# One 2 MB transfer of weights cut into four of eight rows and one of 96, once in a decode kernel

## The chip, the cores and the metric

The kernel runs on one core of one Trainium2 chip. The metric is the device time of one execution in microseconds; the time before is the median of three runs.

## The reference

Two identical layers, each a block of attention over a cached context and a gated feed-forward network, for a batch of two with one new token each. Everything is float32.

```python
x = x + attention(layernorm(x), k_cache, v_cache, wq, wo)   # layer 0
x = x + reglu(layernorm(x), W_gate, W_up, W_down)
x = x + attention(layernorm(x), k_cache, v_cache, wq, wo)   # layer 1, the same arrays again
x = x + reglu(layernorm(x), W_gate, W_up, W_down)
# attention: 32 query heads on 8 kv heads, 32768 cached positions, head size 128
#   scores = q k^T / sqrt(128); p = softmax(scores); o = p v; out = o @ wo
# x [2, 1, 512], k_cache and v_cache [2, 8, 32768, 128], wq [512, 4096], wo [4096, 512]
# reglu: gate = h @ W_gate, up = h @ W_up, (relu(gate) * up) @ W_down, inner size 1792
```

The keys and values are 268 MB each, and both layers read all of them.

## The kernel before

The sixteen pairs of batch element and kv head are walked one after another, each in one *lap*. A lap's keys and values come as four halves, two of k and two of v, each a tile of 128 rows by 16384 floats (8.39 MB; 64 KB a row). Three slots `X`, `Z`, `Y` of that size in the store `arena` hold them; a slot is loaded again when TensorE (PE) has used what was in it.

Layer 0 walks the pairs upwards, layer 1 downwards. In a lap (`lap` in the code) PE first multiplies the second half of the values of the pair before (`values`, into `acc`), then the keys of its own pair (`keys`, into `scores`, named `pair` in the profile), then comes the softmax, then the first half of its values. Between the keys stand small matmuls by which the finished head goes through its part of the weights `wo` into `op` (`head_out`, `project`).

Those weights are the "way out". A tile of 2 MB, 128 rows by 4096 floats (16 KB a row), holds them for two kv heads; it lies at `WO_AT` and is called `weights` and `other` by halves. In laps 3, 7 and 11 of layer 0 (counted from 0, so `i % 4 == 3`; the last lap is excluded) and at three places in layer 1, `fetch_out` loads such a tile. GpSimd (POOL) copies one half over the other in the laps between. The first and last weights come in tiles of half the size.

All loads but x's are issued by SyncE (SP) in the order in which the code names them. SP waits where a transfer would overwrite what is still read, so what stands behind it on SP waits too. Every transfer has a *lane*, a semaphore that tells of its landing: `slot...` for the halves, `wo` for these weights, and otherwise the next of sixteen (`lane0` to `lane15`). A recorder (`Tape`) works out the waits from the regions that are read and written. A k half that goes into the first slot names `weights` as well (`also`), so its issue waits until the weights before it have landed; later readers of the weights then need no wait of their own. PE, VectorE (DVE) and ScalarE (ACT) run the laps as a hardware loop; SP's transfers are written out one by one.

x itself comes as two transfers of four rows by 128 floats on ACT's queue, at the start. At the end of a layer stand the feed-forward network's weights (`wgu`, `wd`), loaded in pieces through a ring or into free slots; at the end of the program the last pieces of `wd` land, PE multiplies, DVE adds to `xq` and SP stores it to `out`.

The profile names tiles and lines by the recorder: nearly all operations have line 214, so groups are told apart by their tiles.

Of the kernel before, what the change touches and what calls it, by code (L numbers as in the profile page):

```python
# [11 lines left out]
P = 128  # L12
# [9 lines left out]
EPS = 1e-5  # L22
QZ = 60
NLAYER = 2

# [5 lines left out]
LANES = 16  # L33
# [11 lines left out]
P_AT, MT_AT, ACS_AT, WO_AT = FLOW, FLOW + 2 * D, FLOW + 2 * D + 32, FLOW + 3 * D + 32  # L45
WO = 4 * D
# [262 lines left out]
def attention_reglu_decode(nc, hold, x, k, v, wq, wo, wgu, wd, out):  # L309
    tape = Tape(nc)  # L310
    pe, dve, act, pool, sp = map(tape.engine, ("tensor", "vector", "scalar", "gpsimd", "sync"))

    def sbuf(name, width):
        return hold.enter_context(nc.sbuf_tensor(name, [P, width], F32))[:, :]
# [4 lines left out]
    arena = sbuf("arena", ARENA)  # L319
# [9 lines left out]
    def tile(at, width):  # L329
        return arena[:, at : at + width]  # L330
# [8 lines left out]
    turn = [0, FLOW, 0, RING[0]]  # L339
# [13 lines left out]
    def fetch(at, src, lane=None, also=()):  # L353
        t = arena[:, at : at + src.shape[-1]]
        if lane is None:
            lane = f"lane{turn[2] % LANES}"
            turn[2] += 1
        sp.dma_start(t, src, lane=lane, also=also)
        return t

    def half(src, n, h, at, also=()):
        return fetch(at, src[n, h], f"slot{at // ROW}", also)
# [1 line left out]
    def part_of(src, n, h, lo, hi, at):  # L364
        return fetch(at, src[n, h, :, lo * D : hi * D])

    def fetch_out(h, n, t, lane="wo"):
        return fetch(t.offset, wo[:, h * WO : (h + n) * WO], lane)

    dve.memset(xq, 0.0)  # L370
    for b in range(NB):
# [104 lines left out]
    def place_queries(n, step=0):  # L476
        dve.tensor_copy(qz[:, 28 : 28 + REP], moving(lambda turn: bass.AP(
            qT.tensor, qT.offset + (1 + n) * REP + turn * (step * REP), [qT.ap[0], [1, REP]])))
# [8 lines left out]
    def soft_max(scores=scores):  # L487
        m1, nm, rs = own(0), own(1), own(2)
        dve.tensor_reduce(m1, scores, AX.XY, ALU.max)
        mt = tile(MT_AT, 32)  # L490
        dve.tensor_scalar_mul(mt, pair, m1)
        pe.matmul(small[0][:, :32], same, mt, start=True, stop=True)
        dve.tensor_reduce(nm, small[0][:, :32], AX.X, ALU.max, negate=True)
        act.activation(tile(P_AT, 2 * D), scores.rearrange("p a b -> p (a b)"), AF.Exp, bias=nm, scale=1.0, accum_out=rs)

    def soft_tail():
        pT, p = tile(PT_AT, 2 * D), tile(P_AT, 2 * D)
        for B in range(2):
            dve.transpose(pT[:, B * D : (B + 1) * D], p[:, B * D : (B + 1) * D])
        pe.matmul(small[1][:, 0:1], same, own(2), start=True, stop=True)  # L500
        dve.reciprocal(own(3), small[1][:, 0:1])
# [11 lines left out]
    def evacuate(split=True):  # L513
        acs = tile(PT_AT if split else ACS_AT, D)
        w = P if split else D
        for t in range(0, D, w):
            dve.tensor_scalar_mul(acs[:, t : t + w], acc[:, t : t + w], own(3))
        return acs

    def head_out(b, acs, weights=None):  # L520
        for t in range(4):
            pe.matmul(small[0][:, :REP], acs[:, t * P : (t + 1) * P], selh[:, 4 * t : 4 * t + 4], start=t == 0, stop=t == 3)
        if weights is not None:
            project(weights)
            dve.memset(oT, 0.0)
        dve.tensor_copy(moving(lambda turn: bass.AP(oT.tensor, oT.offset + (turn + b) % NB, [oT.ap[0], [NB, REP]])), small[0][:, :REP])
# [67 lines left out]
    dve.tensor_reduce(total[:, :1], xq, AX.X, ALU.add)  # L594
    for L in range(NLAYER):
        last = L == NLAYER - 1
        step = -1 if last else 1
# [7 lines left out]
        def keys(h, t, first=0, scores=scores):  # L605
            for e in range(0, t.shape[-1] // D, 8):
                k_blocks(h + e, t[:, e * D : min(t.shape[-1], (e + 8) * D)], first, scores)
                yield e

        def values(lo, t, first=False, final=False):  # L610
            n = t.shape[-1] // D
            for e in range(0, n, 8):
                v_blocks(lo + e, lo + min(e + 8, n), t[:, e * D : min(e + 8, n) * D], first and e == 0, final and e + 8 >= n)

        def lap(i, second, k_first):

            values(HALF, second or half(v, seq[i - 1], 1, b), False, True)
            evacuate(False)
            for e in keys(0, k_first or half(k, seq[i], 0, a, (weights,) if i > L else ())):
                if e == 8:  # L620
                    head_out(1, tile(ACS_AT, D), weights)
            if not last and i == NG - 1:
                pool.tensor_copy(tile(RING[1], KEPT), tile(a, KEPT))
            for _ in keys(HALF, half(k, seq[i], 1, c)):
                pass
            soft_max()
            soft_tail()
            values(0, half(v, seq[i], 0, a), True)
            place_queries(seq[L] + step, step)
            if i % 2 == 1 and i > 1 and (last or i + 1 < NG):  # L630
                h = seq[i] // NB
                if h == 0:
                    fetch_out(h, 1, weights)
                elif i % 4 == 3:
                    fetch_out(h - last, 2, tile(WO_AT, 2 * WO))
                else:
                    pool.tensor_copy(weights, other)

# [7 lines left out]
        if last:  # L646
            n, e = divmod(KEPT, D)

            def again(col):
                return a + col - KEPT if col < REST * D else RING[0] + LENT + col - REST * D  # L650

            for lo, hi in AGAIN:
                fetch(again(lo), k[seq[0], 0, :, lo:hi])
            k_blocks(0, tile(RING[1], n * D), NT // 2, gu)
            k_blocks(n, tile(RING[1] + n * D, e), NT // 2, gu, (0, e))
            k_blocks(n, tile(again(KEPT), D - e), NT // 2, gu, (e, D))
            for lo in range(n + 1, HALF):
                for _ in range({12: 3, REST: 2, 26: 2}.get(lo, 0)):
                    warm(448)
                if lo == REST + 4:  # L660
                    put_back(LENT, STASH)
                k_blocks(lo, tile(again(lo * D), D), NT // 2, gu)
            ready = {1: (tile(b, ROW), half(k, seq[1], 0, a))}
            fetch_out(seq[0] // NB, 1, weights)
            warm(448)
            warm(448)
            soft_max(gu)
            soft_tail()
            values(0, tile(c, ROW), True)
            place_queries(seq[1])  # L670
        else:
            ready = {0: (tile(b, ROW), None)}
            fetch_out(0, 1, weights)
            dve.memset(tile(PT_AT, 2 * D), 0.0)
            nothing(acc, True)
        for i in tape.laps(range(L, NG), 1):
            lap(i, *ready.pop(i, (None, None)))
        nothing(op, False)
        combine()
        n = seq[NG - 1]  # L680
        for lo, hi in ENDING if last else FLOWN:
            t = fetch(b + lo * D, v[n, 1, :, lo * D : hi * D])
# [44 lines left out]
```

## Time and profile before

| | |
|---|---|
| time, median of 3 runs | 2556.62 us (2556.6 to 2557.2) |
| the profiled execution: time, span | 2556.55 us, 2555.2 us |
| PE busy, share of the span | 1335.5 us, 52% |
| DVE, ACT, POOL busy | 157.0, 60.4, 18.2 us |
| bytes moved, mean rate | 1103.29 MB, 432 GB/s |
| the 2 MB loads of `wo`, issue to landing | 6 of them, 31.5 us (median) |

The page shows busy time by engine and, in a section of its own, by DMA queue: q1 is SP's, q10 is ACT's (x), q8 and q14 fetch instructions. A queue's share is the time that its packets took, as a share of what the 16 DMA engines have in that stretch; it can pass 100% where packets reach over the window's edge. A packet is one row (up to 64 KB) or the four bytes that tell of the end. The views of queues and engines can be asked for any window of the span. No view names the DMA engine that carried a packet.

### The profile page before, as it was taken

The page shows a single profiled execution, that of the slowest core. Times are in us where ns is not written, and L with a number is a line of the kernel's source. Part 1 is how long each engine was busy: PE and PEld are TensorE (multiplying, and loading weights), DVE is VectorE, ACT ScalarE, POOL GpSimd, SP SyncE. Part 2 cuts the span into 40 slices and gives each one's busy share as a digit, 9 for nine tenths or more (in the row PEclk, how much of TensorE's full clock was granted, in tenths as well). Part 3 has the DMA queues.
Part 4 walks back from the last instruction along what each step waited for, and adds up shares of the span by engine and source line. Part 5 has one row for each costly group of instructions (what it writes and reads, how often), then busy time and mean ns, then how long its engine had stood idle before and what let it go on. Part 6 is the DMA issues. An engine that isn't in the chain of part 4 may idle for free.

```text
span 2555.2 us, 20572 instructions
## 1 busy us (share of the span) xinstructions
PE 1335.5 (52%) x9542; PEld 366.1 (14%) x9542; DVE 157.0 (6%) x409; ACT 60.4 (2%) x82; POOL 18.2 (1%) x25
## 2 busy tenths in 40 slices
PE   4554545455444554455586554455445554455456
PEld 1111111111111111111121111111111111111112
DVE  1000000000000000000111000000000000000001
ACT  0000000000000000000000000000000000000000
POOL 0000000000000000000000000000000000000000
PEclk9677777777777777777798777777767777777778
DMA  9999999999999999999999999999999999999999
GB/s 425 429 440 429 427 441 430 440 430 431 436 430 440 430 438 429 430 440 430 425 423 440 434 435 432 431 435 435 434 433 431 436 433 435 432 432 435 433 435 389
DMA packets 27248, 1103.29 MB, mean 432 GB/s; under 512 B 3033, under 2 KB 3169, under 8 KB 8033
## 3 DMA queue, kind: packets, MB, share of 16 engines
q1 hardware_dynamic: 27216, 1103.06, 99.9%
q8 instruction: 12, 0.20, 0.0%
q14 instruction: 4, 0.02, 0.0%
q10 hardware_dynamic: 16, 0.00, 0.0%
HBM read 1102.99 MB, written 0.07 MB: 432 GB/s over the span
## 4 chain that ended last, share of the span: by engine, by line
DMA 73%; PE 26%; issue 0%; SPq 0%; DVE 0%; ACT 0%; ACTq 0%
DMA arena<-k 37%; DMA arena<-v 34%; PE acc L214 12%; PE pair L214 11%; DMA arena<-wd 1%; PE small L214 1%; PE op L214 1%; DMA arena<-wq 1%; DMA arena<-wgu 1%; SPq L214 0%; DVE stat L214 0%; DVE arena L214 0%; DVE xq L214 0%; ACT arena L214 0%; ACTq L295 0%
## 5 line engine op out<-in xcount | busy, mean ns | idle before, releaser
L214 PE MATMUL acc<-arena 128*16 128x512 f32 (+2 forms) x4288 | 612.1, 726 | 531.8 <-DMA arena<-v 522.0
L214 PE MATMUL pair<-arena,qz 128*32 128x512 f32 x4098 | 590.7, 730 | 557.5 <-DMA arena<-k 557.5
L214 PEld LDWEIGHTS pair<-arena,qz 128*32 128x32 f32 x4098 | 151.5, 131 | 987.0 <-issue 697.2
L214 PEld LDWEIGHTS acc<-arena 128*16 128x16 f32 (+1 forms) x4288 | 136.8, 112 | 970.6 <-issue 595.5
L214 ACT ACTIVATE arena<-pair,stat 128x1024 f32<-128x1024 f32 x32 | 35.7, 1114 | 2388.1 <-DVE stat L214 2388.1
L214 DVE TENSOR_SCALAR arena<-acc,stat 128x512 f32<-128x512 f32 (+1 forms) x39 | 25.5, 667 | 1051.3 <-PE acc L214 1051.3
L214 DVE TENSOR_REDUCE stat<-pair 128x1 f32<-128x1024 f32 x32 | 39.2, 1225 | 633.5 <-PE pair L214 633.5
L214 DVE STREAM_TRANSPOSE arena<-arena 128x512 f32<-128x512 f32 (+1 forms) x68 | 43.4, 674 | 40.8 <-ACT arena L214 40.7
L214 PE MATMUL small<-stat,cst 128*128 128x1 f32 (+1 forms) x72 | 16.6, 300 | 48.7 <-ACT arena L214 48.7
L214 PE MATMUL small<-arena,cst 128*128 128x32 f32 x64 | 13.1, 286 | 51.6 <-DVE arena L214 51.6
L214 PEld LDWEIGHTS small<-cst,arena 128*128 128x128 f32 x264 | 32.1, 191 | 28.7 <-issue 27.0
L214 PE MATMUL small<-cst,arena 128*128 128x4 f32 x264 | 35.0, 256 | 0.5 <-DVE arena L214 0.5
L214 PE MATMUL op<-arena,oT 128*2 128x512 f32 (+1 forms) x312 | 34.4, 526 | 0.4 <-DVE oT L214 0.3
L214 DVE MEMSET oT<- 128x8 f32 x33 | 2.1, 65 | 513.4 <-PE op L214 513.4
L214 POOL COPY arena<-arena 128x2048 f32<-128x2048 f32 (+1 forms) x7 | 13.5, 1923 | 2191.2 <-PE op L214 2046.7
L214 PE MATMUL op<-arena 128*32 128x448 f32 (+1 forms) x128 | 22.7, 573 | 3.0 <-DMA arena<-wq 1.4
L214 PEld LDWEIGHTS small<-stat,cst 128*128 128x128 f32 x72 | 13.6, 236 | 56.9 <-ACT arena L214 52.2
L214 PEld LDWEIGHTS small<-arena,cst 128*128 128x128 f32 x64 | 9.5, 188 | 80.5 <-DVE arena L214 80.5
L214 ACT ACT_TABLE_LOAD x16 | 20.5, 1283 | 11.4 <-DMA xq<-x 11.1
L214 PE MATMUL acc<-cst 128*32 128x448 f32 (+1 forms) x48 | 18.3, 480 | 0.0
L214 PE MATMUL small<-cst,stat 128*128 128x2 f32 x8 | 1.7, 286 | 18.6 <-DVE stat L214 18.1
L214 PE MATMUL small<-arena 128*32 128x128 f32 x224 | 9.0, 277 | 3.1 <-DVE arena L214 1.7
(63 smaller groups left out, 98.6 us busy)
## 6 DMA issues: line engine op xcount, KB each, us to landing
arena<-wo SPq DMA_DIRECT2D x6, 2048.0 KB, 31.5
arena<-v SPq DMA_DIRECT2D x2, 4096.0 KB, 37.4
arena<-wq SPq DMA_DIRECT2D x14, 512.0 KB, 6.4
arena<-wgu SPq DMA_DIRECT2D x10, 448.0 KB, 6.7
arena<-wo SPq DMA_DIRECT2D x4, 1024.0 KB, 25.3
arena<-wgu SPq DMA_DIRECT2D x1, 3584.0 KB, 44.6
arena<-wgu SPq DMA_DIRECT2D x2, 1792.0 KB, 48.9
arena<-v SPq DMA_DIRECT2D x2, 1536.0 KB, 41.3
```

The lines of the kernel that those rows point to most:

```text
L214: ins = getattr(engine, op.call)(*args, **op.kw)
```

## The change

In layer 0's lap 3 (the fourth), the 2 MB of `wo` come as five transfers: rows 0 to 7, 8 to 15, 16 to 23, 24 to 31, and rows 32 to 127. Each has a lane of its own out of the sixteen instead of the lane `wo`. The other loads of `wo` stay as they were.

```diff
+FEW = (0, 8), (8, 16), (16, 24), (24, 32), (32, P)
...
-    def fetch_out(h, n, t, lane="wo"):
-        return fetch(t.offset, wo[:, h * WO : (h + n) * WO], lane)
+    def fetch_out(h, n, t, lane="wo", rows=True):
+        src = wo[:, h * WO : (h + n) * WO]
+        if rows:
+            return fetch(t.offset, src, lane)
+        for lo, hi in FEW:
+            sp.dma_start(arena[lo:hi, t.offset : t.offset + src.shape[-1]], src[lo:hi, :], lane=f"lane{turn[2] % LANES}")
+            turn[2] += 1
...
                 elif i % 4 == 3:
-                    fetch_out(h - last, 2, tile(WO_AT, 2 * WO))
+                    fetch_out(h - last, 2, tile(WO_AT, 2 * WO), rows=last or i != 3)
```

On SP's queue, from the first half of lap 3's keys (with the waits of each in brackets; `tensor_done` is PE's semaphore), it stood before:

```order
L214 DMA arena<-k 128x16384
L214 DMA arena<-v 128x16384 [waits tensor_done]
L214 DMA arena<-wo 128x4096
L214 DMA arena<-v 128x16384
L214 DMA arena<-k 128x16384 [waits wo_done,tensor_done]
```

and now:

```order
L215 DMA arena<-k 128x16384
L215 DMA arena<-v 128x16384 [waits tensor_done]
L215 DMA arena<-wo 8x4096 x4
L215 DMA arena<-wo 96x4096
L215 DMA arena<-v 128x16384
L215 DMA arena<-k 128x16384 [waits lane2_done,lane3_done,lane1_done,lane4_done,lane0_done,tensor_done]
```

Between the two halves of v stand five transfers instead of one, and the next lap's first half of k waits for five lanes where it waited for `wo`. As five of the sixteen lanes are used here, each later transfer that takes the next lane has one whose number is five higher; on PE at the end of layer 0, for example, it stood before:

```order
L214 MATMUL op<-arena,cst 2x128 [waits vector_done]
L214 MATMUL op<-arena,cst 2x128 x3
L214 MATMUL acc<-arena 16x512 [waits lane0_done]
L214 MATMUL acc<-arena 16x512 x15
L214 MATMUL acc<-arena 16x512 [waits lane1_done]
```

and now:

```order
L215 MATMUL op<-arena,cst 2x128 [waits vector_done]
L215 MATMUL op<-arena,cst 2x128 x3
L215 MATMUL acc<-arena 16x512 [waits lane5_done]
L215 MATMUL acc<-arena 16x512 x15
L215 MATMUL acc<-arena 16x512 [waits lane6_done]
```

Only the names of the semaphores have changed there; PE, DVE, ACT and POOL have the same instructions in the same order, with as many waits.

## The prediction

> **What bounds the kernel now.** I read the page's shares and chain first, then the DMA queues by stretches, then the last four microseconds in small windows, since a kernel whose transfers never pause is decided by whoever moves the last byte. The page's span, queue and chain of work:
>
> ```profile
> span 2555.2 us, 20572 instructions
> ...
> q1 hardware_dynamic: 27216, 1103.06, 99.9%
> ...
> DMA 73%; PE 26%; issue 0%; SPq 0%; DVE 0%; ACT 0%; ACTq 0%
> ```
>
> Queue q1 (SP's transfers) keeps the 16 DMA engines busy for 99.9% of the span. The 26% of PE in the chain is work done while other transfers pass. The same queues in three stretches, 2 to 1230, 1230 to 1400 and 1400 to 2500 us:
>
> ```profile
> DMA packets 9591, 531.95 MB, mean 433 GB/s; under 512 B 1064, under 2 KB 1072, under 8 KB 1072
> ...
> q1 hardware_dynamic: 9572, 531.89, 100.1%
> q8 instruction: 3, 0.05, 0.0%
> ...
> q1 hardware_dynamic: 7085, 72.57, 100.6%
> q8 instruction: 6, 0.10, 0.2%
> q14 instruction: 2, 0.02, 0.0%
> ...
> DMA packets 8509, 476.91 MB, mean 434 GB/s; under 512 B 944, under 2 KB 944, under 8 KB 944
> ...
> q1 hardware_dynamic: 8509, 476.91, 100.2%
> ```
>
> There is no pause anywhere, not even between the layers (1230 to 1400). So engines never wait for one another: an engine that falls behind stays behind until the end. One engine moves 434 / 16 = 27.1 GB/s. What can make them unequal is queue q8, instructions fetched in packets of 16 KB, each on one engine. The window from 38 to 39 us holds one of them:
>
> ```profile
> q8 instruction: 1, 0.02, 5.7%
> ```
>
> 5.7% of 16 engines for 1 us is 0.91 us of one engine. How unequal they are by the end shows in windows of 0.5 us (last two columns: share of the engines that is busy, GB/s):
>
> ```profile
> 2549.00:2549.50 0.50, 0.50 (x20) 0.50 (x24) 0.00 (x0) 0.00 (x0) 0.00 (x0) 1.00 0.87 336
> 2549.50:2550.00 0.50, 0.50 (x23) 0.48 (x14) 0.00 (x0) 0.00 (x0) 0.00 (x0) 1.00 0.71 279
> 2550.00:2550.50 0.50, 0.50 (x12) 0.15 (x7) 0.00 (x0) 0.00 (x0) 0.00 (x0) 1.00 0.56 221
> 2550.50:2551.00 0.50, 0.50 (x17) 0.37 (x10) 0.00 (x0) 0.00 (x0) 0.00 (x0) 1.00 0.50 176
> 2551.00:2551.50 0.50, 0.50 (x12) 0.21 (x7) 0.00 (x0) 0.00 (x0) 0.00 (x0) 1.00 0.21 82
> 2551.50:2552.00 0.50, 0.50 (x18) 0.50 (x18) 0.00 (x0) 0.00 (x0) 0.00 (x0) 1.00 0.20 78
> 2552.00:2552.50 0.50, 0.50 (x15) 0.30 (x9) 0.00 (x0) 0.00 (x0) 0.00 (x0) 1.00 0.06 21
> ```
>
> Divide the last column by 27.1: 12.4 engines, 10.3, 8.2, 6.5, then 3.0, 2.9 and 0.8. Eight engines are through by about 2550.4; five more by about 2551; three work on until 2552.0 + 0.8 x 0.5 / 3 = 2552.13. The kernel's end hangs on these three, as the end of the chain of work shows:
>
> ```profile
> 2522.87 29.84 DMA arena<-wd
> 2552.70 0.04 issue
> 2552.75 0.47 PE small L214 x8
> 2553.22 0.02 issue
> 2553.24 0.29 DVE xq L214
> ```
>
> The last transfer is issued 29.84 us before it counts as landed at 2552.70; all behind it is 2.5 us and fixed. So I ask of the change one thing: by how much does it move the last engine's end? Eleven of the twelve q8 packets come before these windows; if they go round eight engines, three get two and five get one, which fits 3, 5 and 8. That is inference: no view names an engine. Followed end to start, the single packets of the trace put the first three fetches on other engines than the four that carry x's rows. I use this only to weigh two cases below.
>
> **The change part by part.** *What a row costs.* The stretch from 317.5 to 319 us holds nothing but rows of the 2 MB transfer itself:
>
> ```profile
> DMA packets 38, 0.62 MB, mean 415 GB/s; under 512 B 0, under 2 KB 0, under 8 KB 0
> ...
> q1 hardware_dynamic: 38, 0.62, 96.7%
> ```
>
> 0.967 x 16 x 1.5 us / 38 = 0.61 us for a row of 16 KB. Before, each engine carries 8 of the 128 rows.
>
> *How eight rows spread.* No transfer of this program has eight rows. The nearest is x's, four rows of 512 bytes on ACT's queue; here are the windows 7 to 8 us (its rows) and 9 to 11 us (its ends):
>
> ```profile
> DMA packets 20, 1.05 MB, mean 1051 GB/s; under 512 B 0, under 2 KB 4, under 8 KB 4
> ...
> q10 hardware_dynamic: 4, 0.00, 0.7%
> ...
> DMA packets 20, 1.05 MB, mean 524 GB/s; under 512 B 4, under 2 KB 4, under 8 KB 4
> ...
> q10 hardware_dynamic: 4, 0.00, 0.1%
> ```
>
> Four rows leave four end packets (under 512 B), while 1064 - 8 = 1056 = 66 x 16 come from the big transfers of the first stretch: one end packet for each engine that takes part. So I read: four rows, four engines; eight rows, eight engines; 96 rows, sixteen engines with six each. If it is the same eight every time, these carry 4 + 6 = 10 rows and the others 6. Eight engines end 2 x 0.61 = 1.22 us later, eight 1.22 us earlier. [...]
>
> *Whether eight neighbouring rows go in at full speed.* This is the term that decides, and no row shows it. The two long stretches above run at 433 and 434 GB/s, and that is 16 equal shares: either each engine has a cap of 27.1 GB/s, or each of 16 doors into the store has. If engines, a transfer of eight rows takes 0.61 us and there is no further cost. If doors, 128 rows over 16 doors is eight rows a door; then eight neighbours share, at worst one door: 8 x 0.61 = 4.88 us a transfer. Between lie two engines to a door (1.22) and four (2.44). The four transfers follow each other on the same eight engines, so the extra over 4 x 0.61 is 0, 2.44, 7.32 or 17.1 us. The row nearest to the truth would be x's, but its 512 bytes are too short to tell. I take the middle of the two inner steps, (2.44 + 7.32) / 2 = 4.9 us, and keep both ends: abreast, four would share for the full 7.32, but the engines arrive apart and partly use a door in turn.
>
> [...]
>
> *The sum.* The eight early engines' last is 2552.13 - 2550.4 = 1.75 us ahead of the end. If they are the eight that get the extra: -1.75 + 1.22 + 4.9 = +4.4 us. Against the profiled execution (2556.55 us with a span of 2555.2, 0.07 below the median of 2556.62) that makes 2560.9; I say 2561.0 on the median.
>
> *Issue and waits.* SP in the fourth lap, with its queue's waits (280 to 345 us) and the chain there:
>
> ```profile
> 289.80 0.33 SPq L214 DMA_DIRECT2D arena<-v  x1
> 290.17 0.43 SPq L214 DMA_DIRECT2D arena<-wo  x1
> 290.65 0.44 SPq L214 DMA_DIRECT2D arena<-v  x1
> ...
> SPq L212 <- DMA arena<-wo: 30.3, 1, 30.3
> SPq L214 <- PE acc L214: 4.6, 1, 4.6
> ...
> 289.80 26.71 DMA arena<-v
> ...
> 325.94 0.02 issue
> 325.96 34.09 DMA arena<-k
> ```
>
> Four more issues of some 0.4 us delay the second v by 1.6 us; the v ahead of it is issued at 289.80 and in flight for 26.71 us, so the queue does not run dry: nothing. Behind the five waits that replace one stands the next lap's pair of k. Today the landing of wo ends first and PE's matmuls end last, 4.6 us later. If wo lands up to 7.32 + 1.22 us later on some engines, the wait on it may be the last by up to 4 us. Then k is issued later; but k spends 34.09 us from issue to landing, of which its own 8.39 MB at 434 GB/s take 19.3, so 14.8 us of queue cover it. Nothing, unless the lag exceeds that. The later lanes only change names on PE and DVE, with no wait added: nothing. The 32 additional end packets are four on each of eight engines; x's four take 0.001 x 16 x 2 us together, 0.008 us each, so 0.03 us: nothing.
>
> **The rivals.**
>
> 1. *Doors, and four engines abreast at each: slower.* The full 7.32: -1.75 + 1.22 + 7.32 = +6.8 us, 2563.4. For it: nothing else in the program separates the engines before the fourth lap than a few fetches of 0.91 us, so they come to the small rows close together. Against: what comes apart once stays apart, and then a door is used in turn. It decides (over 5.1 us) once the extra passes 5.1 + 0.5 = 5.6 us.
> 2. *Engines are the cap, and the eight are the early ones.* -1.75 + 1.22 = -0.5 us: 2556.1; the three late ones give up two rows each and the last of the early eight ends the kernel. For it: three engines alone hold the end today, and x's engines are not those of the first fetches. Against: nothing shows the absence of doors. Perfect balance bounds it: the busy shares above sum to 3.11 x 0.5 us = 1.56 us beyond 2549, so 2550.56 for all, 1.6 us less than today.
> 3. *Engines are the cap, and one of the three late ones is among the eight.* It gets two rows more: +1.22 us, 2557.8. With doors as well the worst is 1.22 + 7.32 = +8.5 us: 2565.1.
> 4. *The change does not unbalance anything:* each eight rows take another eight engines. 2556.6. x's two transfers are too small to say.
> 5. *One door or one engine for all eight rows*, 32 rows in a line: -1.75 + 1.22 + 17.1 = +16.6 us, 2573. x's four end packets speak against the one engine, nothing against one door.
>
> **How the numbers follow.** Doors used partly in turn, my forecast: 0.27, 2561.0, with a range of its own from 2558.5 (-1.75 + 1.22 + 2.44 = +1.9) to 2561.7 (an extra of 5.6, where rival 1 decides). Rival 1: 0.23; rival 2: 0.22; rival 3: 0.16, doors included; rival 4: 0.07; rival 5: 0.05. About 0.2%, 5.1 us, is what a measurement of this kernel can tell from no change. Beyond it lie rivals 1 and 5 and the part of rival 3 with doors, 0.03: 0.31. Faster by that much nothing can make it, since balance gives 1.6 us: 0.01. The rest, 0.68, is within. The range takes in rival 2, a little better than worked out (2555.8), and the worst of shared doors (2565.2); rival 5 and edges are left out, under 0.1.
>
> **What would show it.** In the window of the small rows, after 314 us, packets of 16 KB on q1: at 0.61 us each engines are the cap; at 1.2 to 2.4 us doors are shared, and q1's share of the window divided by packets tells directly. In the last windows: more than three engines at the end, and a longer tail, if the eight were held up; a shorter tail with the three ending 1.22 us earlier for rival 2; the same three 1.22 us later for rival 3. The wait of SP on the lanes should be last, not PE's, only with doors. I am wrong if the lag does not last to the end, that is, if q1's share shows a pause, or if the rate of the middle stretches changes.

## The result and the profile after

The changed kernel takes 2565.61 us (median of 6 runs, 2565.14 to 2568.1), the kernel before 2556.70 us beside it (6 runs, 2556.55 to 2557.3). The ratio is 1.0036, with a 95% interval of 1.0023 to 1.0049: 8.9 us more, slower by more than 0.2%. The forecast was 2561.0, its range ended at 2565.2. The profiled execution of the changed kernel took 2565.14 us with a span of 2563.8, 8.6 more than the span before. From its page come the span, the queue and the chain's first line:

```profile
span 2563.8 us, 20578 instructions
...
q1 hardware_dynamic: 27248, 1103.07, 99.9%
...
DMA 74%; PE 25%; issue 0%; SPq 0%; DVE 0%; ACT 0%; ACTq 0%; DVEq 0%
```

The share of q1 is 99.9% as before, and its packets are 27248 - 27216 = 32 more: four transfers with eight end packets each. By this share nothing has happened. The engines are as busy as ever and move less in the same time. Where, the windows of 6 us from 314 us on show (last two columns: DMA share, GB/s), first of the kernel before, then of the changed one:

```profile
314.00:320.00 6.00, 3.35 (x16) 0.74 (x20) 0.00 (x0) 0.00 (x0) 0.00 (x0) 0.50 1.13 483
320.00:326.00 6.00, 5.90 (x52) 1.43 (x44) 0.00 (x0) 0.00 (x0) 0.00 (x0) 0.91 0.90 390
326.00:332.00 6.00, 0.00 (x0) 0.00 (x0) 0.00 (x0) 0.00 (x0) 0.00 (x0) 0.66 1.13 492
```

```profile
314.00:320.00 6.00, 1.01 (x8) 0.37 (x12) 0.00 (x0) 0.00 (x0) 0.00 (x0) 0.50 0.91 202
320.00:326.00 6.00, 6.00 (x43) 1.36 (x36) 0.00 (x0) 0.00 (x0) 0.00 (x0) 0.69 1.30 314
326.00:332.00 6.00, 2.39 (x24) 0.47 (x16) 0.00 (x0) 0.00 (x0) 0.00 (x0) 0.88 0.75 281
```

The three windows average 455 GB/s before and 266 after, at about the same share. A packet is simply longer. The queues of the changed kernel in 314.5 to 316 us and in 316 to 319.5 us:

```profile
DMA packets 33, 0.29 MB, mean 197 GB/s; under 512 B 15, under 2 KB 15, under 8 KB 15
...
q1 hardware_dynamic: 33, 0.29, 95.3%
...
DMA packets 71, 0.80 MB, mean 229 GB/s; under 512 B 22, under 2 KB 22, under 8 KB 22
...
q1 hardware_dynamic: 71, 0.80, 102.5%
```

The packets under 512 B are ends, so 18 and 49 are rows: 0.953 x 16 x 1.5 / 18 = 1.27 us for a row of 16 KB, and 1.025 x 16 x 3.5 / 49 = 1.17, where it had been 0.61. The second window reaches into the 96 rows: they are as slow as the small transfers. So are the rows of v that come next. In the single packets of the trace, 27 of v's 64 KB rows here take longer than their usual 2.42 us, up to 4.96, and lose 41 us of engine time together; the 128 rows of wo lose 128 x (1.139 - 0.611) = 68 us. Spread over 16 engines that is 109 / 16 = 6.8 us each. The engine that ends last loses more. Followed from end to start, its packets are a row of v (1.3 us longer than usual), ten rows of wo where it had eight (two more at 0.61: 1.2; the four small ones 1.9 longer, the six of the 96 3.3 longer) and one more row of v (0.4 longer): 8.1 us, of the 8.6 that the span grew. No view names an engine, so this is put together from the packets' times.

SP's timeline in lap 3, with the chain there:

```profile
289.93 1.74 SPq L215 DMA_DIRECT2D arena<-wo  x5
291.71 0.43 SPq L215 DMA_DIRECT2D arena<-v  x1
330.13 0.82 SPq L215 DMA_DIRECT2D arena<-k  x2
...
291.35 38.70 DMA arena<-wo
...
330.13 38.39 DMA arena<-k
```

The 96 rows land 38.70 us after their issue, SP's wait for them is now the last, and the next lap's k is issued at 330.13 in place of 325.96. That k lands at 330.13 + 38.39 = 368.52; before it landed at 325.96 + 34.09 = 360.05. The difference, 8.5 us, is the whole loss but for 0.1: it arises between 314 and about 332 us, and the 2200 us behind it only carry it along. The last windows of the changed kernel:

```profile
2558.00:2558.50 0.50, 0.50 (x28) 0.50 (x20) 0.00 (x0) 0.00 (x0) 0.00 (x0) 1.00 0.58 225
2558.50:2559.00 0.50, 0.50 (x14) 0.25 (x9) 0.00 (x0) 0.00 (x0) 0.00 (x0) 1.00 0.69 234
2559.00:2559.50 0.50, 0.50 (x16) 0.25 (x15) 0.00 (x0) 0.00 (x0) 0.00 (x0) 1.00 0.35 135
2559.50:2560.00 0.50, 0.50 (x12) 0.34 (x4) 0.00 (x0) 0.00 (x0) 0.00 (x0) 1.00 0.17 66
2560.00:2560.50 0.50, 0.50 (x18) 0.39 (x17) 0.00 (x0) 0.00 (x0) 0.00 (x0) 1.00 0.08 29
2560.50:2561.00 0.50, 0.50 (x21) 0.38 (x10) 0.00 (x0) 0.00 (x0) 0.00 (x0) 1.00 0.04 16
```

Divided by 27.1 they are 8.3, 8.6, 5.0, 2.4, 1.1 and 0.6 engines: a tail of some 3 us, hardly longer than before. It isn't eight engines that end late; all sixteen have moved by 8 to 9 us.

### The profile page after: what moved, and what is told of

It is laid out like the page before. It is cut to its first block, busy times and chain, and to the rows that moved or that the text cites. A ratio compares the mean times of both kernels' runs of the same rounds, so it can differ in the third digit from the quotient of the medians.

```text
span 2563.8 us, 20578 instructions
## 1 busy us (share of the span) xinstructions
PE 1341.5 (52%) x9542; PEld 367.8 (14%) x9542; DVE 157.0 (6%) x409; ACT 60.4 (2%) x82; POOL 18.2 (1%) x25
## 3 DMA queue, kind: packets, MB, share of 16 engines
q1 hardware_dynamic: 27248, 1103.07, 99.9%
## 4 chain that ended last, share of the span: by engine, by line
DMA 74%; PE 25%; issue 0%; SPq 0%; DVE 0%; ACT 0%; ACTq 0%; DVEq 0%
DMA arena<-k 38%; DMA arena<-v 32%; PE pair L215 11%; PE acc L215 11%; DMA arena<-wgu 2%; DMA arena<-wo 2%; PE small L215 1%; PE op L215 1%; DMA arena<-wq 1%; DMA arena<-wd 0%; SPq L215 0%; DVE arena L215 0%; DVE stat L215 0%; DVE xq L215 0%; ACT arena L215 0%
## 5 line engine op out<-in xcount | busy, mean ns | idle before, releaser
L215 PE MATMUL acc<-arena 128*16 128x512 f32 (+2 forms) x4288 | 618.4, 733 | 533.5 <-DMA arena<-v 526.9
```

Of the source, the lines that this page charges most:

```text
L215: ins = getattr(engine, op.call)(*args, **op.kw)
```

## The experiments

Theory at first, an assumption carried on from the prediction: rows that lie side by side in the store and come at the same time wait for one another, as at a door that lets in no more than one engine's rate (27.1 GB/s), and rows beside them wait too. No view shows such a door. The rivals: few rows are slow by themselves; the unbalance (10 rows against 6); the number of transfers with their issue and waits; and, later, places in the device memory in place of the store. All kernels use one helper, which issues one transfer for each entry of a list (first row, step, number of rows, first and last column); a small addition to the recorder lets those of one group (`apart`) go without waits for one another:

```diff
+    def in_parts(at, src, parts, apart=None):
+        for first, step, n, c0, c1 in parts:
+            t = arena[:, at : at + src.shape[-1]]
+            sp.dma_start(rows_of(t, first, step, n, c0, c1), rows_of(src, first, step, n, c0, c1), lane=f"lane{turn[2] % LANES}", apart=apart)
+            turn[2] += 1
...
-                    fetch_out(h - last, 2, tile(WO_AT, 2 * WO))
+                    if last or i != 3:
+                        fetch_out(h - last, 2, tile(WO_AT, 2 * WO))
+                    else:
+                        in_parts(WO_AT, wo[:, h * WO : (h + 2) * WO], PARTS, "parts")
```

Below mostly `PARTS` alone is shown. Times are medians, compared with the kernel before on the same chip; the groups ran on four chips, and the kernel before took 2556.7 to 2556.8 us on each.

**Every fourth row in the small transfers.**

```diff
+PARTS = tuple((r, 4, 8, 0, 4096) for r in range(4)) + ((32, 1, 96, 0, 4096),)
```

> Lap 3's 2 MB still come as four transfers of eight rows and one of 96, but each of the four takes every fourth row of the first 32 (0, 4, .. 28; then 1, 5, ..), so that no two rows of one transfer are neighbours. [...] Rival, transfers of few rows are slow by themselves, whichever rows: as the change, +8.9, 2565.6. Rival, only the two additional rows count: -0.5 or +1.2.

2563.28 us, ratio 1.0026 [1.0016, 1.0037]: +6.6. Its queues in 314.5 to 316 us and in 318 to 319.5 us:

```profile
DMA packets 56, 0.56 MB, mean 371 GB/s; under 512 B 22, under 2 KB 22, under 8 KB 22
...
q1 hardware_dynamic: 56, 0.56, 95.1%
...
DMA packets 26, 0.36 MB, mean 240 GB/s; under 512 B 4, under 2 KB 4, under 8 KB 4
...
q1 hardware_dynamic: 26, 0.36, 96.0%
```

The 34 small rows of the first window take 0.951 x 16 x 1.5 / 34 = 0.67 us each: few rows are not slow by themselves, if they lie apart. The 22 rows of the second, of the 96, take 0.960 x 24 / 22 = 1.05 us. The +6.6 fits neither rival (+8.9; -0.5 or +1.2): the larger part of the price sits where I had not looked.

**32 rows and 96 rows.**

```diff
+PARTS = ((0, 1, 32, 0, 4096), (32, 1, 96, 0, 4096))
```

> The same 2 MB as two transfers, rows 0 to 31 and 32 to 127; both use all sixteen engines, two and six rows each, so there is no unbalance and no transfer of eight rows. [...] Rival, few rows are slow by themselves: at most a third of the change's loss, below +2. Rival, only unbalance counts: 0, 2556.7.

2563.71 us, 1.0027 [1.0016, 1.0039]: +7.0. The queues in 315 to 318 us:

```profile
DMA packets 47, 0.49 MB, mean 164 GB/s; under 512 B 17, under 2 KB 17, under 8 KB 17
...
q1 hardware_dynamic: 47, 0.49, 98.7%
```

0.987 x 16 x 3 / 30 = 1.58 us a row. Without any transfer of eight rows, and without unbalance as I take it (32 and 96 are multiples of 16), most of the loss is there, more than either rival allowed (below +2, and 0).

**More rows beside the kernel before, apart and neighbouring.** The load of wo is whole again; in each of laps 2 to 13 four transfers of eight rows by 896 floats go into columns that nothing reads.

```diff
+            if not last and 2 <= i < 14:
+                in_parts(FREE_AT, wo[:, :896], PARTS, f"parts{i}")
...
+PARTS = tuple((r, 4, 8, 0, 896) for r in range(4))        # every fourth row
+PARTS = tuple((r, 1, 8, 0, 896) for r in range(0, 32, 8)) # neighbouring rows
```

> Before, plus rows that nothing reads: in each of the laps 2 to 13 of layer 0 four transfers of eight rows of 896 floats (3.5 KB) into unused columns, each of every fourth row of 0 to 31. 48 rows on each of the engines that take part, 3584 / 16384 x 0.61 = 0.133 us each, 6.4 us in all. All theories: 6.4 us if the engines that take part include one of the three late ones, 6.4 - 1.75 = 4.6 if they are the early eight; the last windows show eight engines at the end. Rival, few rows are slow by themselves (about 2 us for each transfer, as in the change): over +50 us.

> As the run with additional rows that lie apart, with the same number, size and engines, but each transfer takes eight neighbouring rows (0 to 7, 8 to 15, 16 to 23, 24 to 31). [...] Rivals (engines are the cap, or few rows are slow by themselves): the same time as with rows apart.

Apart: 2564.19 us, 1.0028 [1.0018, 1.0037], +7.5. Neighbouring: 2572.98 us, 1.0058 [1.0041, 1.0075], +16.3. The same bytes on the same number of engines cost 8.8 us more where the rows are neighbours. The first stretch (100 to 1200 us) of each tells it too, 432 and 429 GB/s at the same share:

```profile
100.00:1200.00 1100.00, 557.36 (x3856) 148.69 (x3860) 56.82 (x140) 34.84 (x42) 5.68 (x3) 0.72 1.00 432
...
100.00:1200.00 1100.00, 543.48 (x3804) 145.57 (x3808) 56.81 (x140) 34.84 (x42) 5.68 (x3) 0.73 1.00 429
```

The single rows are only a little longer (0.161 against 0.150 us); what grows is v's rows beside them, which lose some 128 us of engine time against 37. The one with rows apart also ran at two levels, half of its runs near 2562.3 and half near 2565.5, so it doesn't say how much a late engine's extra rows cost to better than 3 us.

**96 rows more, and 128 rows more.** In the same place, with the same number of bytes in both.

```diff
+PARTS = ((32, 1, 96, 0, 896),)
+PARTS = ((0, 1, 128, 0, 672),)
```

> The term that the prediction left out, by itself and twelve times over: the wo load of lap 3 is whole again, and in each of laps 2 to 13 one transfer of 96 rows (32 to 127) by 896 floats is added, into columns that nothing reads. Each engine carries 6 rows more a lap, 72 in all. A row of this size took 0.132 us by the rate of one engine and 0.14 to 0.15 us where it had its door alone (every fourth row). 96 rows free of sharing, as the prediction had it: 72 x 0.132 to 0.15 = +9.5 to +10.8 us, the same as the kernel with the same bytes in 128 rows. Theory (96 rows share doors, each row 1.9 times as long, as 1.18 us stood to 0.61 in lap 3): +18 to +21 us, and rows of 0.25 to 0.28 us in the records. Rival (the 96 rows were slow in lap 3 only because of what went before them): as free of sharing.

> The control to it: the same bytes in the same laps, as 128 rows by 672 floats. Each engine carries 8 rows more a lap, 96 in all, of 2688 bytes: 0.099 us by the rate of one engine. Theory and rival alike: 96 x 0.099 to 0.112 = +9.5 to +10.8 us, rows of about 0.1 us. If it too comes to +18 us, the price is one of rows or of the place of the extra transfer and not of doors.

96 rows: 2589.43 us, 1.0136 [1.0113, 1.0159], +32.7. 128 rows: 2566.84 us, 1.0040 [1.0026, 1.0054], +10.1, as worked out from bytes alone. Their stretches from 100 to 1200 us, in this order:

```profile
100.00:1200.00 1100.00, 548.94 (x3798) 146.30 (x3798) 55.20 (x135) 32.34 (x39) 5.68 (x3) 0.72 1.00 427
...
100.00:1200.00 1100.00, 548.71 (x3852) 147.60 (x3856) 56.82 (x140) 34.84 (x42) 5.69 (x3) 0.74 1.00 433
```

So 96 rows are not free, by themselves and in any lap. They cost more than I had expected of the theory (+18 to +21): the rows are 0.198 us on average and not 0.25 to 0.28, but v's rows beside them lose some 151 us of engine time, which I had left out. (The 0.14 to 0.15 us that I started from were measured with every fourth row, 0.150 on average; that such a row has a door alone is the theory's wording and was not shown.) With the 96-row transfers' own 228 us that is 379 / 16 = 23.7 us for each engine, and the profiled run's span is 25.7 us longer than before. That run was the shortest of four (2582.24; the longest 2595.54); what the longer ones add no trace shows.

**Halves, and every second row.** Two transfers of 64 rows in lap 3.

```diff
+PARTS = ((0, 1, 64, 0, 4096), (64, 1, 64, 0, 4096))  # halves
+PARTS = ((0, 2, 64, 0, 4096), (1, 2, 64, 0, 4096))   # every second row
```

> Lap 3's 2 MB as two transfers, rows 0 to 63 and 64 to 127. Both have as many rows on each of 16 engines (four), so nothing is unbalanced. [...] Rival (only transfers of few rows, or those that unbalance the engines, cost): 0 to +1 us, rows of 0.61 us.

> [...] Rival (any transfer of other than 128 rows is slow, by its way of being issued): the same as the halves.

Halves: 2564.05 us, 1.0029 [1.0018, 1.0040], +7.3. Every second row: 2556.68 us, 1.0000 [0.9990, 1.0009], 0.0. The queues in 315 to 318 us, first of the halves, then of every second row:

```profile
DMA packets 28, 0.43 MB, mean 142 GB/s; under 512 B 2, under 2 KB 2, under 8 KB 2
...
q1 hardware_dynamic: 28, 0.43, 94.0%
...
DMA packets 92, 1.25 MB, mean 415 GB/s; under 512 B 16, under 2 KB 16, under 8 KB 16
...
q1 hardware_dynamic: 92, 1.25, 97.0%
```

0.940 x 48 / 26 = 1.74 us a row against 0.970 x 48 / 76 = 0.61. The two kernels have as many transfers, rows and bytes; only which rows go together differs, and that is worth 7.4 us. 64 neighbouring rows (1.74 us) are no faster a row than the 32 above (1.58).

**Each part of the change alone.** First only the 96 rows, then only the four small transfers; the rest of that tile is zero, written by DVE at the start.

```diff
+    dve.memset(arena[:, WO_AT : WO_AT + 2 * WO], 0.0)
...
+PARTS = ((32, 1, 96, 0, 4096),)                           # 96 rows alone
+PARTS = tuple((r, 1, 8, 0, 4096) for r in range(0, 32, 8)) # four small alone
```

> In lap 3 only the 96 rows (32 to 127) are loaded, in one transfer; rows 0 to 31 of these weights are left out (zeros are written there at the start by DVE), so the output is that of other weights, and each engine carries two rows less than before: 2 x 0.61 = 1.22 us less on all sixteen. If the 96 rows are free of sharing, as the prediction had it: -1.2 us, rows of 0.61 us. Theory: every fourth row of the first 32 went at full speed and that kernel still took 6.6 us more, of which two more rows on a late engine are 1.22; the 96 rows then cost 5.4 by themselves, with the rows of v beside them: 5.4 - 1.22 = +4.2 us (+3 to +5.5), rows of 1.0 to 1.3 us.

> The other part by itself: only the four transfers of eight neighbouring rows; the 96 rows are left out (zeros there). Eight engines carry four rows instead of eight, the others none. The late engines among the eight set the end: without sharing 4 x 0.61 - 8 x 0.61 = -2.44 us. With the row time of the changed kernel, 1.18 us: 4 x 1.18 - 4.88 = -0.2 us, and up to 2 us more if rows of v beside them are slowed: -0.2 to +1.8. If the eight were the early engines, the end would move by what the late ones lose, as much as -4.9.

96 alone: 2560.87 us, 1.0016 [1.0006, 1.0026], +4.1, though 0.5 MB less is moved. Four small alone: 2558.82 us, 1.0008 [0.9999, 1.0018], +2.1, though 1.5 MB less is moved. Their queues in 315 to 318 us, in this order:

```profile
DMA packets 44, 0.64 MB, mean 213 GB/s; under 512 B 5, under 2 KB 5, under 8 KB 5
...
q1 hardware_dynamic: 44, 0.64, 92.3%
...
DMA packets 25, 0.20 MB, mean 66 GB/s; under 512 B 13, under 2 KB 13, under 8 KB 13
...
q1 hardware_dynamic: 25, 0.20, 38.3%
```

Rows of 0.923 x 48 / 39 = 1.14 us and of 0.383 x 48 / 12 = 1.53 us. (A window counts the packets that start in it: the 38.3% are eight engines' small rows, while the other engines were on rows of v begun before.) The first came out as the theory had it (+4.2): the 96 rows cost 4.1 + 1.22 = 5.3 us more than their bytes, v's rows beside them included. The second is slightly above its bound of +1.8, and what I had too small is v's part: on the engine that ends last, followed from end to start, the four small rows take 1.11 us each, less than the 1.18 that I took, but the rows of v before and behind them take 4.33 and 2.95 us in place of 2.42.

**Five transfers by columns, and four of every fourth row.**

```diff
+PARTS = tuple((0, 1, 128, c, c + 512) for c in range(0, 2048, 512)) + ((0, 1, 128, 2048, 4096),)  # columns
+PARTS = tuple((r, 4, 32, 0, 4096) for r in range(4))                                              # every fourth of 128
```

> Five transfers on the same five lanes, with the same waits behind them, but cut by columns: four of 128 rows by 512 floats and one of 128 rows by 2048. Every transfer has every row. All theories of doors and of balance: 0 (-0.3 to +0.3 us). Rival (the number of transfers, their issue on SP or the five waits cost something): +1 us or more.

> [...] If only doors count: 0, rows of 0.61 us, as with every second row. If two rows an engine are too few for the spread (two engines at a door): rows of up to 1.22 us and +2 to +5 us. The 32 neighbouring rows had 1.6 to 1.85 us a row.

2556.72 us, 1.0000 [0.9991, 1.0010], and 2556.66 us, 1.0000 [0.9991, 1.0010]: no difference in either. The second one's queues in 315 to 318 us:

```profile
DMA packets 109, 1.25 MB, mean 415 GB/s; under 512 B 33, under 2 KB 33, under 8 KB 33
...
q1 hardware_dynamic: 109, 1.25, 97.4%
```

0.974 x 48 / 76 = 0.62 us a row, with 32 rows a transfer. Five transfers, their issue on SP and the five waits cost nothing, and neither do transfers of 32 or 64 rows that are stepped over all 128.

**Store or device memory.** So far neighbouring rows of the store came from neighbouring rows of the device memory, 64 KB apart there. In four kernels the two are chosen apart (`FROM` gives first row and step in the device memory), with rows of 896 floats in laps 2 to 13 as above.

```diff
-        for first, step, n, c0, c1 in parts:
+        for (first, step, n, c0, c1), (f, s) in zip(parts, FROM):
...
+PARTS, FROM = tuple((r, 1, 8, 0, 896) for r in range(0, 32, 8)), tuple((r, 4) for r in range(4))   # eight next in store
+PARTS, FROM = tuple((r, 4, 8, 0, 896) for r in range(4)), tuple((r, 1) for r in range(0, 32, 8))   # eight next in source
+PARTS, FROM = ((0, 1, 64, 0, 896), (64, 1, 64, 0, 896)), ((0, 2), (1, 2))                          # halves in store
+PARTS, FROM = ((0, 2, 64, 0, 896), (1, 2, 64, 0, 896)), ((0, 1), (64, 1))                          # halves in source
```

> The four transfers of eight rows by 896 floats in laps 2 to 13 once more (apart in both memories +7.5 us, neighbouring in both +16.3): now eight neighbouring rows of the store, filled from every fourth row of the device memory. Theory (doors into the store): as neighbouring in both, +14 to +18. Rival (the device memory: rows 64 KB apart meet at one place there): as apart, +6 to +9.

> The reverse: every fourth row of the store, filled from eight neighbouring rows of the device memory. Theory (store): +6 to +9. Rival (device memory): +14 to +18. If both this and the other lie at +7.5, it needs neighbours in both; if both at +16, either suffices.

> In the same laps two transfers of 64 rows by 896 floats, four rows an engine each, 96 rows more an engine in all: 96 x 0.132 to 0.15 = +12.7 to +14.4 us if nothing is shared. Here rows 0 to 63 and 64 to 127 of the store, filled from every second row of the device memory. Theory (store): well above, +30 to +60 us (in lap 3 the halves' rows were 2.1 to 2.8 times as long, and v's rows beside them were slowed as well). Rival (device memory): +12.7 to +14.4.

> The reverse: every second row of the store, filled from rows 0 to 63 and 64 to 127 of the device memory. Theory (store): +12.7 to +14.4 us. Rival (device memory): +30 to +60 us.

Neighbours in the store: 2572.45 us, 1.0056 [1.0040, 1.0073], +15.7, and for the halves 2605.72 us, 1.0189 [1.0172, 1.0206], +49.0. Neighbours in the device memory: 2563.39 us, 1.0025 [1.0015, 1.0035], +6.6, and 2569.67 us, 1.0050 [1.0033, 1.0067], +12.9. The stretch from 100 to 1200 us of the two with halves, store and then source:

```profile
100.00:1200.00 1100.00, 533.31 (x3692) 142.17 (x3692) 53.50 (x131) 32.34 (x39) 5.68 (x3) 0.71 1.00 421
...
100.00:1200.00 1100.00, 549.38 (x3828) 146.84 (x3832) 56.82 (x140) 34.82 (x42) 5.68 (x3) 0.73 1.00 433
```

Both pairs agree: it is the place in the store. Neighbours in the device memory cost no more than rows apart in both (+6.6 against +7.5) or than the bytes alone (+12.9 against the +12.7 to +14.4 worked out).

**Apart, but elsewhere; and every second row.** The small transfers beside the kernel before once more.

```diff
+PARTS = tuple((64 + r, 4, 8, 0, 896) for r in range(4))     # apart, rows 64 to 95
+PARTS = tuple((r, 2, 8, 0, 896) for r in (0, 1, 16, 17))    # every second row
```

> The four transfers of eight rows by 896 floats, every fourth row, now rows 64 to 95 in place of 0 to 31 (+7.5 us there). [...] If only neighbours matter: +6 to +9 again. [...]

> [...]

Rows 64 to 95, every fourth: 2571.93 us, 1.0057 [1.0041, 1.0074], +15.2. Every second row of the first 32: 2569.64 us, 1.0048 [1.0032, 1.0065], +12.9. The first of these corrects the theory. Its rows lie as far apart as those that cost +7.5, and cost as much as neighbours (+16.3): to lie apart isn't enough, and where in the store they lie counts too. A reading that fits is that a row is held up unless it is brought by the engine that brings it in a whole transfer. No view names the engine of a row, so this is inferred from the times and not shown. The first stretch of that kernel, in a run that was the longest of four (2576.28 us):

```profile
100.00:1200.00 1100.00, 538.26 (x3800) 143.94 (x3800) 56.82 (x140) 34.82 (x42) 5.68 (x3) 0.74 1.00 428
```

428 GB/s, where the same rows from 0 to 31 left 432. The second lies between the two ends, +7.5 and +16.3, but its interval goes from +8.2 to +16.6, so it gives no size for a step of two.

## Why the prediction was wrong

*That the queue never pauses and the last engine decides* was nearly right. The share is 99.9%, and from 1400 to 2500 us the rate is 433 GB/s after 434. But at the layer boundary the engines that were ahead ran short of work for a moment, which the prediction had excluded. The window from 1290 to 1300 us, before and after:

```profile
1290.00:1300.00 10.00, 8.14 (x44) 1.32 (x44) 0.00 (x0) 0.63 (x1) 0.00 (x0) 1.00 1.03 420
...
1290.00:1300.00 10.00, 8.53 (x80) 3.37 (x81) 1.82 (x11) 0.00 (x0) 0.56 (x1) 1.00 0.95 358
```

In the single packets, fewer than 16 are in flight there for 9.1 us of engine time; in the kernel before this doesn't happen between 1230 and 1400 us. Some engines lose their lead there; the slowest loses nothing, and the end follows it.

The prediction also left out PE, which is busy through every one of the last windows, before and after. The changed kernel's chain has no transfer in it from the landing of `wgu` at 2499.80 + 44.22 = 2544.02 on, only PE and, for about 1 us, DVE; the last load of weights into PE waits for `wd` for 0.29 us:

```profile
2499.80 44.22 DMA arena<-wgu
...
2561.36 0.47 PE small L215 x8
```

Here PE and the last transfer end together. What the end would have gained had the engines ended earlier, as in rival 2, no run shows.

*Eight engines take the eight rows*: right by the 32 additional ends. That they are the same eight each time no view shows; the order of the packets has four small rows on the engine that ends last. *Doors, not engines, are the cap*: an engine's rate alone is not the cap, and it is the place in the store that counts (neighbours there +15.7 and +49.0, neighbours in the device memory +6.6 and +12.9). That there are doors, and how many engines meet at one, no run shows; the runs showed 1.27 us a row with neighbours and 0.67 with every fourth row, in the same window (314.5 to 316 us). And the prediction asked only how many of the eight meet, while rows 64 to 95 cost about as much (+15.2) as neighbours (+16.3) though no two of the eight are neighbours: by the reading above, inferred and not shown, it would count as well which engine brings a row.

*The extra of the small transfers, 4.9 us*: too large for the rows themselves. At 1.18 us a row (1.033 x 32 / 28, from 316.5 to 318.5 us) they lose 4 x (1.18 - 0.61) = 2.3, just under the 2.44 of the prediction's first step. But the prediction counted only these rows, and v's rows beside them are held up too: by themselves, with four rows instead of eight, the small transfers cost 2.1 + 4 x 0.61 = 4.5 us. That this lies near 4.9 is luck.

*The 96 rows as sixteen engines with six rows each, at 0.61 us*: this is the step that failed. The question of doors was put to the small transfers alone, and the 96 rows got the price of a row in a transfer of 128; they took 1.05 us each in the kernel with every fourth row and 1.14 alone. They cost 5.3 us more, v's rows beside them included, and twelve such transfers cost 32.7 us where the same bytes in 128 rows cost 10.1. Why they are slower, the runs don't show: no view tells how the 96 rows are dealt out to the engines.

*The eight as the early engines, -1.75 us* (1.73 by its own figures): this failed as well. The engine that ends last carries ten rows, not six. 96 alone, +4.1, with four more rows on eight engines at 1.18 us each gives 4.1 + 4.7 = 8.8, as measured (8.9); with four at 0.65, the mean of the first 32 rows in the kernel with every fourth row, 4.1 + 2.6 = 6.7, as that kernel measured (6.6). The additional rows count in full. In the single packets two of the three late engines are among the eight. The intervals of these differences are some 2.5 us to each side, so that this is well supported by four medians and the packets, but not settled.

*Issue, lanes and waits cost nothing*: right. SP's wait on wo came to be the last and k was issued 4.2 us later (I had said up to 4), with no pause behind it; five transfers by columns cost 0.0.

The sum, mended: two more rows 1.22, small transfers 2.3, the 96 rows 5.3 with v's rows, credit 0: 8.8 us against 8.9 measured. It fits so well because v's rows are counted once, with the 96; with the small transfers as measured alone (4.5) it would be 11.0, since in each run alone the rows of v before and behind are held up anew. Rival 3's worst case came near with 2565.1 by luck: it had the late engine rightly, but 7.32 for the small transfers and nothing for the 96.

## What to carry to other kernels

When a load that keeps all DMA engines busy is cut by rows, ask of every piece, the large rest too, which rows of the store go together in it: cuts by columns, or into every second or fourth row of all 128, cost nothing here (0.0 us), while two halves of neighbouring rows cost 7.3 us once on 2 MB. Don't look for such a loss in the queue's share, which stays at 99.9%; divide share by packets, or look at GB/s in the windows around the transfer. And let the price include the rows of the transfers beside it, which are held up too (here v's lost 41 us of engine time beside 68 for those of wo).

## What the runs showed of the hardware

While the slow rows are under way, the other rows in flight slow as well. In the kernel with every fourth row, at 320 us, rows of 16 KB take 1.12 to 1.25 us and rows of v, 64 KB, 4.7 to 4.9: both about twice their own time (0.61 and 2.42). With the four small transfers alone, rows of v on the engines that take no part lengthen to 5.4 us. So the loss is larger than that of the slow rows themselves. For the halves in twelve laps, 96 rows an engine at 0.132 to 0.15 us would be +12.7 to +14.4 us if nothing were held up, and +49.0 were measured (+44 at the least). Why engines that take no part are slowed, the runs don't show; no view names an engine.

A row in a transfer of 64 rows (every second) or 32 rows (every fourth) takes 0.61 and 0.62 us, the same as in one of 128 (0.61). How such rows are dealt out to the engines no view shows; by the reading above they would come to the engines that bring them in a whole transfer, which is inferred from the times alone.
